# Attention and a gated feed-forward on one core: activated rows stored from ScalarE's queue, k's squares moved ahead, one sum of w_in moved back

## The chip, the core and the metric

The kernel runs on one core of a Trainium2 chip. The metric is device time in microseconds (us). The core has TensorE (PE: matmuls, with PEld for its weight loads), VectorE (DVE), ScalarE (ACT), GpSimd (POOL) and SyncE (SP), which here only issues DMAs. Each engine takes its instructions strictly in the order of the program; between engines they wait on semaphores. PSUM is the memory that TensorE writes its results to, SBUF the one that the other tensors are in.

## What is computed

Two blocks follow each other, all in float32:

```python
q_n, k_n = rmsnorm(q, g_q), rmsnorm(k, g_k)            # q, k, v: 8 batches x 12 heads x 448 x 64
scores = q_n @ k_n.T / sqrt(64)
attn = softmax(scores)
x = (attn @ v) bridged to (8*448, 12*64)               # 3584 tokens x 768
h = x @ w_in                                           # 768 x 2048
out = (h * sigmoid(h)) @ w_out                         # 2048 x 768
```

The rmsnorm divides each row of 64 by the root of its mean square (plus 1e-6) and multiplies by the gains.

## The kernel before

**Couples.** Attention goes in 24 couples of two head pairs (four heads) each, three couples per batch. Couples 0 to 5 are the first group of two batches (GROUP = 6). From couple 6 on, the feed-forward's first matmul of the group before runs between the steps of attention: couples 6 to 11 carry batches 0 and 1, couples 12 to 17 batches 2 and 3, and so on. The last group's feed-forward and the second matmul come when attention is over. From couple LATE = 12 on, q and k are loaded in another layout; some of its steps begin with couple 10 (LATE - 2).

**Visit and between.** For each couple c the program first writes `visit(c)` (L1397): the matmuls of the scores (L712), their exps on ScalarE (L717, with the norm of k as the scale), the products with v (L749), and the division of couple c - 1's result (L808). Then comes `between(c)` (L1463): the transposes of couple c + 1's q and k through TensorE (L629, L647) with their copies by ScalarE (L633, L649); the column sums of the exps, first by adds on VectorE (L763) and then by matmuls with ones (L783), their reciprocals (L792) and the DMAs that spread them (L799, L801); the norms of couple c + 2; and the filler. Exp and SiLU lie in different tables of ScalarE, so each change costs an ACT_TABLE_LOAD; `between` ends with a tiny exp (L1524) that loads exp's table again.

**The filler.** The first matmul of the feed-forward is done in blocks of seven products, as Strassen does in Winograd's form (class `Seven`, L888): for each block of 256 columns of w_in and two batches, products named 1, 2, 6, 5, 7, 3, 4 in that order (blocks 0 and 1 of the first group have 1 and 2 done earlier). A product is three matmul steps (L902) into one PSUM bank of two that are used in turn; each shows as two records in the trace. Products 1 and 5 are copied out by ScalarE (L910, L920), the others are added to something by VectorE (L857); GpSimd adds product 5 to two sums (L922, L923). A finished block leaves two rows of 128 x 896 in `stage`. When the next block has begun, `activate` (L1038) applies SiLU to both rows (L1040) and `save` (L934) stores them to `hidden` in DRAM from SyncE's queue. There are three row buffers in turn, so a later block writes a row again once its store has landed.

**fill.** `fill(others, prompt)` (L1334) writes a share of the filler's steps and deals the pieces of `others` out between them, evenly over the steps; pieces of `prompt` go after every third step. What is left comes at the end. `between` calls it twice: the first half with the late adds (L763, four pieces), rounding steps of w_in and the norms of k; the second half with rounding steps, the norms of q, and the transposes, sums and reciprocals as `prompt`. The order in `others` is the order in which the engines get the pieces.

**Norms of k** (`normalise`, L812, pieces 2 and 3): ScalarE squares one half of k's rows into a scratch tile (L467), VectorE sums them per row (L468); both halves use the same scratch, so the second square waits for the first sum; then L492 on VectorE and a power on GpSimd (L496).

**w_in.** Its 24 pieces are loaded by SyncE (L85), opened by ScalarE (L100, L101), and rounded by VectorE (L123, L126, L130) and GpSimd (L134), some in `halves` of couples, some in visits. For each of four chunks of w_in four sums (`sum_w_in`, L954, VectorE, L854 and L857 on tile W) are made ahead of the blocks that need them; `sums_halves` says in which half of which couple: `sums_halves[8]` is the first half of couple 10, index 2 (c - 6) + half.

Of the kernel before, what the change touches and what calls it, by code (L numbers as in the profile page):

```python
# [535 lines left out]
def bounded(  # L536
# [8 lines left out]
    others = ctx.enter_context(ExitStack())  # L545
# [4 lines left out]
    GROUP, LATE = z.NPAIR, z.LATE  # L550
# [3 lines left out]
    hidden = dram.tile([z.NF, P, z.B * S], F32, name="hidden")  # L554
# [9 lines left out]
    def piece(n):  # L564
        nonlocal at
        at += n
        return work[:, at - n : at]
# [17 lines left out]
    late = [extra[:, ds(2 * z.NW * S - (i + 1) * n, n)].bitcast(I32) for i in range(2)]  # L585
# [53 lines left out]
    def transpose_k(c):  # L639


        assert z.KB == BANK
        t = ps.tile([P, 2, BANK], F32, name="sc", bufs=2)
        rows = place[f"k{c % 2}"]
        for i in range(2):
            for j in range(z.KEYS + 1 - i):
                nc.tensor.transpose(t[:, i, ts(j, P)], rows[:, ds((z.KA, z.KB)[i] + j * P, P)], ident)  # L647
        columns = t.rearrange("p i s -> p (i s)")[:, 0 : z.NK]
        nc.scalar.activation(kT, columns, AF.Copy, scale=gains)  # L649
        loads["k" if c < LATE - 1 else "quarters"](min(c + 2, LATE))  # L650
# [116 lines left out]
    def sum_up(c):  # L767

        n = D // 2
        early = c < GROUP
        t = bank(S) if c < GROUP - 1 else ps.tile([P, 2, BANK], F32, name="sc", bufs=2)[:, 0, 0:S]
        terms = [(0, lambda: weights(c, 0))]
        if early:
            terms = [(0, lambda: weights(c, LEFT - 1))] + terms + [(1, None)]
        for k, (which, w) in enumerate(terms):
            if k == len(terms) - 2:
                yield  # L780
            for h in range(2):
                for i in range(2):
                    nc.tensor.matmul(  # L783
                        t[ds(h * D + i * n, n), :],
                        ones[:, which + i if which else 0],
                        eleft[:, h] if which else w()[:, i, h],
                        start=(k == 0), stop=(k == len(terms) - 1),
                    )

        def invert(half):  # L790
            rows = ts(half, S // 2)
            nc.vector.reciprocal(out=r[0][:, rows], in_=t[:, rows])  # L792

        def spread():
            mine = [a.rearrange("(h i p) s -> i h p s", h=2, i=2) for a in r]
            queues = (nc.sync, nc.gpsimd if c == GROUP - 1 else nc.sync)
            for h in range(2):
                for i in range(2):
                    queues[h].dma_start(mine[1][i, h], mine[0][1, h])  # L799
            for h in range(2):  # L800
                queues[h].dma_start(mine[0][1, h], mine[0][0, h])  # L801

        yield [lambda: invert(0), lambda: (invert(1), spread())]

    def divide(c, source):
        for i in range(2):
            x = x_of(c, i)
            nc.vector.tensor_tensor(  # L808
                out=x, in0=x if source is None else source[i], in1=r[i], op=ALU.mult
            )  # L810
# [121 lines left out]
        return stages[-1]  # L932

    def save(f, column, t):  # L934
        nc.sync.dma_start(hidden[f, :, ds(column, t.shape[1])], t)


    AHEAD = 2
# [15 lines left out]
    def sum_w_in(i, step):  # L954

        assert room.w_in.rounded >= (i + 1) * z.NW
        summed.add((i, step))
        w = room.chunk(i).rearrange("p (c m r k) -> p c m r k", c=z.NW, m=2, r=2)
        up, low = w[:, 0:HW], w[:, HW:]
        s = room.sums(i).rearrange("p (s c m k) -> p s c m k", s=3, c=HW, m=2)  # L960
        left_sums(
            up[:, :, :, 0], low[:, :, :, 0], up[:, :, :, 1], low[:, :, :, 1],
            s[:, 0], s[:, 1], s[:, 2], (step,),
        )
# [8 lines left out]
    def sum_x(group, c, steps=range(4)):  # L973
        right_sums(*quarters(group, c), *sums_of_x(c), steps)
# [359 lines left out]
    def fill(others=(), prompt=()):  # L1334


        others, prompt, steps, dealt = list(others), list(prompt), 0, 0
        if prompt:
            prompt.pop(0)()
        filler["due"] += filler["share"]  # L1340
        total = max(1, int(filler["due"] / S))
        while filler["due"] > 0:
            step = next(filler["work"], None)
            if step is None:
                break
            filler["due"] -= step
            steps += 1
            if prompt and steps % HW == 0:
                prompt.pop(0)()
            while dealt < min(len(others), len(others) * steps // total):  # L1350
                others[dealt]()
                dealt += 1
        filler["due"] = min(filler["due"], 0.0)
        for other in prompt + others[dealt:]:
            other()
# [8 lines left out]
    def finish():  # L1364
        run(filler["work"])
# [10 lines left out]
    for c in range(GROUP // 2):  # L1376
        halves[2 * (c - GROUP)], halves[2 * (c - GROUP) + 1] = "rr", "o"
    sums_halves = {-6: [(0, 0)], -4: [(0, 1)], -3: [(0, 2)], -2: [(0, 3)]}
    sums_halves[8] = [(3, step) for step in range(4)]
    sums_visits = {GROUP + 1: 1, GROUP + 3: 2}  # L1380

    def weights_in(c, half):
        i = 2 * (c - GROUP) + half
        work = [step_of[step] for step in halves.get(i, "ro" if c < GROUP else "")]
        return work + [lambda a=a: sum_w_in(*a) for a in sums_halves.get(i, ())]
# [8 lines left out]
    def last_two(c):  # L1394
        return [c // GROUP * 2 - 2, c // GROUP * 2 - 1]
# [63 lines left out]
    def run_all(work):  # L1459
        for piece in work:  # L1460
            piece()

    def between(c):  # L1463

        def transposes_and_sums():
            summing = sum_up(c)
            if c < GROUP:
                next(summing)
            if c == GROUP - 1:
                reciprocals = next(summing)  # L1470
                divide(c - 1, None)
                run_all(reciprocals)
                sum_x([0, 1], 0)
                transpose_k(c + 1)
                return
            if c < LATE - 1:
                transpose_k(c + 1)
            reciprocals = next(summing)
            if LATE - 1 <= c < NC - 1:
                reciprocals += [lambda: flip(c + 1, "k"), gain]  # L1480
            if GROUP // 2 <= c < EARLY:
                divide(c - 1, None)
            return reciprocals

        if c < LATE - 1:
            transpose_q(c + 1)
        elif c < NC - 1:
            flip(c + 1, "q")
        if c < GROUP // 2:
            inverting.extend(transposes_and_sums())  # L1490
        elif c == GROUP - 1:
            transposes_and_sums()
        if c >= GROUP and c % GROUP == 0:
            fetched = range(AHEAD) if c == GROUP else ()
            columns = products - 2 * HW * S * len(fetched)
            work = halves_in(last_two(c), range(HF), plain_in, dict(begun), fetched)
            begin(work, columns, 2 * GROUP)
            begun.clear()
        late = add(c, LEFT - 1) + add(c, LEFT) if c >= GROUP else []
        further = normalise(c + 2) if c >= GROUP - 1 else []  # L1500
        fill(late + weights_in(c, 0) + (further[2:] if c >= GROUP else further[:2]))
        prompt = transposes_and_sums() if GROUP // 2 <= c != GROUP - 1 else []
        if prompt and c < GROUP:
            prompt.insert(0, lambda: None)
        if c == GROUP // 2:
            begin(make_ahead([0, 1]), AHEAD * 2 * HW * S, GROUP - 1)
        if c >= LATE - 2:
            if c == LATE - 2:
                prompt.append(pair_up)
            queries = prompt[3:] + [lambda: sum_squares(c + 2)]  # L1510
            fill(weights_in(c, 1), prompt[:3] + [lambda: run_all(queries)])
        else:
            fill(weights_in(c, 1) + (further[:2] if c >= GROUP else []), prompt)
        if c % GROUP == GROUP - 1:
            finish()
            if c == GROUP - 1:
                begun[0] = fetch_ahead([0, 1], 0)
            elif c < NC - 1:
                sum_x([c // GROUP * 2, c // GROUP * 2 + 1], 0, range(2))
        if c >= LATE - 2:  # L1520
            scale(c + 2)
        if GROUP <= c < NC - 1:

            nc.scalar.activation(first, minus_half, AF.Exp)  # L1524
        if c == NC - 1:
            while rounder.load():
                pass
# [236 lines left out]
```

## Time and profile before

| what | us |
|---|---|
| median of three runs (lowest, highest) | 1325.13 (1323.84, 1328.43) |
| the profiled execution: whole time | 1323.7 |
| the profiled execution: span of its instructions | 1321.9 |
| TensorE busy / VectorE busy / ScalarE busy | 1298.3 / 949.2 / 505.2 |
| start of the visit of couple 7, 8, 9, 10, 11, 12 | 155.2, 189.4, 224.6, 257.9, 294.6, 327.2 |
| a store of a row (448 KB) from SyncE: median issue, median time to landing | 0.37, 3.1 |

A row of the timeline gives the start, the duration, the engine, the line, the operation, what is written and read, and in brackets how long the engine had been idle and what ended that. Times are counted from the span's start. In the list of windows each stretch is followed by its length, the busy time of TensorE, of its weight loads, of VectorE, ScalarE and GpSimd with the number of instructions, the clock granted to TensorE as a share of full speed, the mean busy share of the 16 DMA engines, and GB/s. The chain lists, in order of time, the pieces of work that released each other up to the last instruction.

### The profile page before, as it was taken

To read this page: it belongs to the slowest core of one execution; us is meant where nothing else is said; L and a number is where in the kernel's file an instruction comes from. 1 tells how busy PE (TensorE), PEld (TensorE's weight loads), DVE (VectorE), ACT (ScalarE), POOL (GpSimd) and SP (SyncE) were. 2 spreads that over 40 slices of the span, in tenths; PEclk is the share of its full clock that TensorE was granted. 3 is DMA by queue.
4 is the path that set the end of the run, shared out by engine and by line. 5 is a ranking of instruction groups with operands and counts; after the bars stand their busy time and mean duration, and the time that the engine had idled before them with its cause. 6 is when DMAs were issued, how large, how long until landed. Compare 5 with 4: busy or idle time off the path is not lost.

```text
span 1321.9 us, 19806 instructions
## 1 busy us (share of the span) xinstructions
PE 1298.3 (98%) x7193; PEld 829.3 (63%) x7193; DVE 949.2 (72%) x1629; ACT 505.2 (38%) x886; POOL 361.5 (27%) x230
## 2 busy tenths in 40 slices
PE   8989999999999999999999999999999999999998
PEld 4433444444444444444444455558999999999998
DVE  6888776776755555855554686698978787878785
ACT  7966656645545545454444253410100000001000
POOL 6756444343334334333420244410000000000000
PEclk9999999999999999999999999999999999999999
DMA  8674337233443444444321367412323232231411
GB/s 232 169 189 110 113 91 209 80 90 91 95 116 91 97 103 107 96 93 117 81 67 67 106 197 259 150 60 76 100 76 106 76 101 90 92 114 63 132 45 39
DMA packets 249439, 144.94 MB, mean 110 GB/s; under 512 B 184292, under 2 KB 233220, under 8 KB 249332
## 3 DMA queue, kind: packets, MB, share of 16 engines
q1 hardware_dynamic: 248672, 142.42, 38.5%
q8 instruction: 59, 0.97, 0.3%
q0 software_dynamic: 352, 0.96, 0.2%
q14 instruction: 48, 0.39, 0.1%
q10 hardware_dynamic: 308, 0.20, 0.1%
HBM read 93.98 MB, written 41.29 MB: 102 GB/s over the span
## 4 chain that ended last, share of the span: by engine, by line
PE 83%; DVE 6%; ACT 4%; DMA 3%; issue 2%; POOL 1%; SPq 1%; ACTq 0%; DVEq 0%; POOLq 0%
PE mm L902 25%; PE alone L1209 23%; PE mm L1209 8%; PE av L749 8%; PE sc L712 7%; PE alone L902 7%; PE alone L1246 2%; PE sc L783 1%; DMA work<-work 1%; DVE work L763 1%; DVE work L792 1%; ACT work L717 1%; PE mm L1246 1%; ACT stage L1040 1%; DMA hidden<-stage 1%
## 5 line engine op out<-in xcount | busy, mean ns | idle before, releaser
L902 PE MATMUL mm<-x,W 128*128 128x448 f32 x612 | 246.7, 546 | 4.7 <-DVE parts L857 2.0
L717 ACT ACTIVATE work<-sc,rms 128x448 f32<-128x448 f32 x324 | 184.8, 634 | 71.9 <-PE sc L712 58.0
L902 PE MATMUL mm<-sums_x,W 128*128 128x448 f32 x480 | 193.4, 543 | 1.5 <-DVE parts L857 1.5
L902 PEld LDWEIGHTS mm<-x,W 128*128 128x128 f32 x612 | 112.3, 190 | 131.1 <-issue 104.3
L712 PE MATMUL sc<-work 64*64 64x448 f32 x1344 | 165.6, 546 | 1.8 <-ACT work L717 1.5
L763 DVE TENSOR_TENSOR work<-work 128x896 f32<-128x896 f32 (+1 forms) x114 | 123.7, 1118 | 50.1 <-PE av L749 49.6
L749 PE MATMUL av<-work,rows 64*64 64x448 f32 x1296 | 154.1, 543 | 3.3 <-ACT av L725 2.2
L902 PEld LDWEIGHTS mm<-sums_x,W 128*128 128x128 f32 x480 | 89.6, 190 | 95.2 <-issue 85.5
L496 POOL TENSOR_TENSOR rms<-rms,minus_half 128x14 f32<-128x14 f32 (+4 forms) x43 | 105.2, 2449 | 149.2 <-DVE rms L492 139.6
L523 POOL DMA_DIRECT2D out_dram<-x x2 | 1.2, 594 | 443.3 <-DVE x L857 443.3
L1209 PE MATMUL alone<-W,rows 128*128 128x192 f32 x610 | 113.0, 326 | 0.0
L749 PEld LDWEIGHTS av<-work,rows 64*64 64x64 f32 x1296 | 57.8, 132 | 75.7 <-issue 35.8
L1209 PEld LDWEIGHTS alone<-W,rows 128*128 128x128 f32 x610 | 101.5, 190 | 0.0
L712 PEld LDWEIGHTS sc<-work 64*64 64x64 f32 x1344 | 53.6, 133 | 74.8 <-ACT work L717 29.2
L922 POOL TENSOR_TENSOR parts<-parts,stage 128x448 f32<-128x448 f32 x31 | 42.1, 1357 | 148.8 <-DVE parts L857 143.1
L688 POOL TENSOR_TENSOR rms<-rms,minus_half 128x28 f32<-128x28 f32 x12 | 57.5, 4794 | 64.1 <-DVE rms L685 57.4
L1209 PE MATMUL alone<-W,work 128*128 128x192 f32 x382 | 72.2, 326 | 0.0
L1040 ACT ACTIVATE stage<-stage 128x896 f32<-128x896 f32 x63 | 57.3, 945 | 23.6 <-DVE stage L857 22.9
L1219 ACT COPY rows<-alone 128x192 f32<-128x192 f32 x33 | 10.5, 319 | 142.1 <-PE alone L1209 78.4
L468 DVE TENSOR_REDUCE rms<-rows 128x8 f32<-128x512 f32 (+2 forms) x56 | 35.9, 640 | 39.1 <-ACT rows L467 37.9
L1209 PEld LDWEIGHTS alone<-W,work 128*128 128x128 f32 x382 | 63.8, 190 | 0.0
L792 DVE RECIPROCAL work<-sc 128x224 f32<-128x224 f32 x38 | 58.6, 1547 | 5.7 <-PE sc L783 5.5
(250 smaller groups left out, 2114.5 us busy)
## 6 DMA issues: line engine op xcount, KB each, us to landing
hidden<-stage SPq DMA_DIRECT2D x63, 448.0 KB, 3.1
work<-hidden SPq DMA_DIRECT2D x21, 1024.0 KB, 5.1
rows<-in_moe_w_out_dram SPq DMA_DIRECT2D x32, 384.0 KB, 3.4
W<-in_moe_w_in_dram SPq DMA_DIRECT2D x22, 512.0 KB, 5.1
work<-work SPq DMA_DIRECT2D x141, 56.0 KB, 2.0
x<-hidden SPq DMA_DIRECT2D x7, 1024.0 KB, 5.6
rows<-in_q_dram SPq DMA_DIRECT2D x96, 56.0 KB, 2.3
rows<-in_k_dram SPq DMA_DIRECT2D x96, 56.0 KB, 2.3
```

Of the source, the lines that this page charges most:

```text
L496: nc.gpsimd.tensor_tensor(out=t, in0=t, in1=half, op=ALU.pow)
L688: nc.gpsimd.tensor_tensor(out=f, in0=f, in1=minus_half.to_broadcast([P, n]), op=ALU.pow)
L712: nc.tensor.matmul(two[ds(half * D, D), h, 0:S], keys[rows, ts(half, D)], qT[rows, pair, :], start=True, stop=True,)
L717: nc.scalar.activation(eleft[:, h] if j == LEFT else weights(c, j)[:, i, h], two[:, h, 0:S], AF.Exp, scale=norm.column(c, i, h, j),)
L749: nc.tensor.matmul(sums[i][ds(h * D, D), :], v, w, start=(j == 0 and step == 1), stop=(j == LEFT - 1 and step == 1),)
L763: nc.vector.tensor_tensor(out=total, in0=total, in1=more, op=ALU.add)
L792: nc.vector.reciprocal(out=r[0][:, rows], in_=t[:, rows])
L902: nc.tensor.matmul(t, self.left(name, s), self.right(name, s), start=s == ends[0], stop=s == ends[1])
L922: nc.gpsimd.tensor_tensor(out=u2, in0=u2, in1=p5, op=ALU.add)
L1040: nc.scalar.activation(t, t, AF.Silu)
L1209: nc.tensor.matmul(t, x[:, i], y, start=i == ORDER[0], stop=i == ORDER[-1])
L1246: nc.tensor.matmul(o, a[:, 2 * i + m, t], right_one(name, i)[:, m], start=n == 0, stop=n == len(steps) - 1,)
```

## The change

Three edits. `save` uses ScalarE's queue where the column is 0, which is the first group, whose blocks are made in couples 6 to 11: sixteen stores. In the first half of couples 6 to 10 the two pieces of k's squares stand ahead of the adds and rounding steps. Of the four sums of w_in's last chunk the fourth goes to the second half of couple 10; empty pieces keep the number of pieces of its first half at ten, and set its place in the second.

```diff
     def save(f, column, t):
-        nc.sync.dma_start(hidden[f, :, ds(column, t.shape[1])], t)
+        queue = nc.scalar if column == 0 else nc.sync
+        queue.dma_start(hidden[f, :, ds(column, t.shape[1])], t)
...
-    sums_halves[8] = [(3, step) for step in range(4)]
+    sums_halves[8] = [(3, step) for step in range(3)]
+    sums_halves[9] = [(3, 3)]
...
-        fill(late + weights_in(c, 0) + (further[2:] if c >= GROUP else further[:2]))
+        others = late + weights_in(c, 0)
+        rest = further[2:] if c >= GROUP else further[:2]
+        others = rest + others if GROUP <= c < LATE - 1 else others + rest
+        if c == LATE - 2:
+            others.append(lambda: None)
+        fill(others)
...
-            fill(weights_in(c, 1), prompt[:3] + [lambda: run_all(queries)])
+            steps = weights_in(c, 1)
+            fill(steps + [lambda: None] * len(steps), prompt[:3] + [lambda: run_all(queries)])
```

The stores on ScalarE stand in its order right behind the SiLU of their row, one between the two SiLUs of a block and one behind them. In couples 6, 7, 9 and 10 both squares of k reach ScalarE ahead of the block's SiLUs; in couple 8 the first does and the second comes behind the two SiLUs and their stores. TensorE's order is the same in both programs.

## The prediction

> **What bounds the kernel now.** I read the page's busy times first, then six windows from the end of one couple's scores to the start of the next couple's, then the chain and the timelines inside them.
>
> ```profile
> PE 1298.3 (98%) x7193; PEld 829.3 (63%) x7193; DVE 949.2 (72%) x1629; ACT 505.2 (38%) x886; POOL 361.5 (27%) x230
> ```
>
> TensorE is the bound: 98%, so all idle time together is 1321.9 - 1298.3 = 23.6 us. The windows of couples 6 to 11 (columns: stretch, then length, then busy time of each engine):
>
> ```profile
> 132.10:155.20 23.10, 22.73 (x83) 11.30 (x79) 19.48 (x29) 13.00 (x19) 8.62 (x7) 1.00 0.33 93
> 166.20:189.40 23.20, 22.58 (x79) 11.34 (x79) 16.72 (x25) 12.84 (x20) 7.35 (x5) 1.00 0.46 128
> 200.40:224.50 24.10, 22.93 (x76) 11.16 (x75) 17.11 (x22) 13.06 (x20) 8.39 (x6) 1.00 0.73 211
> 235.60:257.80 22.20, 22.20 (x76) 11.37 (x75) 16.93 (x22) 12.50 (x20) 7.64 (x5) 1.00 0.28 68
> 269.70:294.60 24.90, 23.28 (x85) 11.57 (x81) 19.87 (x22) 10.29 (x14) 9.55 (x9) 1.00 0.48 111
> 305.60:327.20 21.60, 21.36 (x66) 10.05 (x65) 15.54 (x19) 9.17 (x12) 4.81 (x3) 1.00 0.46 113
> ```
>
> TensorE idles 139.10 - 135.09 = 4.0 us in them; 0.9 us more is idle inside the visits of couples 10 and 12. That is the whole prize. The clock is full (1.00). The largest stall, couple 8, in the chain of waits:
>
> ```profile
> 204.77 1.79 ACT stage L1040 x2
> 206.56 0.08 ACT W L100
> 206.63 5.32 DMA hidden<-stage
> ...
> 212.49 0.64 ACT rows L467
> ...
> 213.15 0.70 DVE rms L468
> ...
> 213.87 0.53 ACT rows L467
> ...
> 215.19 0.88 DVE work L792
> ...
> 216.57 0.57 DVE parts L857
> ```
>
> ScalarE's copy of product 5 (L920) may not write the stage row until its save has landed; k's squares (L467) stand behind it, VectorE's reduces (L468) behind those, and L857, which empties the bank that TensorE wants, behind all. ScalarE at 38% is idle on average, yet at the end of couple 9 it is the chain:
>
> ```profile
> 253.81 1.79 ACT L1040 ACTIVATE stage<-stage 128x896 f32<-128x896 f32 x2
> 255.51 0.66 ACT L100 ACTIVATE W<-W 128x512 int32<-128x512 uint32 x1
> ...
> 257.74 0.61 ACT L467 ACTIVATE rows<-rows 112x512 f32<-112x512 f32 x1
> 259.10 0.63 ACT L467 ACTIVATE rows<-rows 112x512 f32<-112x512 f32 x1 [0.75 <-DVE rms L468]
> 259.75 1.28 ACT L1524 ACT_TABLE_LOAD   x1
> 261.15 1.14 ACT L717 ACTIVATE work<-sc,rms 128x448 f32<-128x448 f32 x2
> ```
>
> Couple 10's scores start at 257.87, their exps only at 261.15, and TensorE stalls at 261.86 for 0.49 us. Exps may start 2.4 us after the scores at no cost: that visit takes 11.85 us with a delay of 3.28, the other visits of couples 6 to 11 take 11.0 with delays near 1.1 to 1.8.
>
> **Yardsticks.** A 3-step product is 6 TensorE records 0.376 apart, 2.26 us. Products alternate between two PSUM banks, so the copy or sum that empties one has one product's time. A stall costs its idle time plus about 0.17 for the drained pipeline and 0.10 at restart. TensorE's order is unchanged by the change; its times move only through waits.
>
> **Part 1, saves on ScalarE's queue.** Sixteen issues leave SyncE (0.32 to 1.36 us each, median 0.37) and go to ScalarE. The trace has five ScalarE issues of other tensors: 0.53, 0.23, 0.54, 0.50, 0.39; I take 0.44, bounds 0.23 and SyncE's 1.24 in couple 8. Each waits for its SiLU, and the second SiLU stands behind the first issue. A pair of SiLUs takes 1.79 now; with two gaps of 0.06, two issues, and the 0.10 of overlap lost, about 2.9: **+1.1 us of ScalarE per pair** (bounds +0.7, +2.7). Queued behind it: L100/L101, k's or q's squares, the table load and the next exps.
>
> There is a second wait. The built program hands out eight landing semaphores in turn, so a transfer waits for the landing of the one eight before it in program order. On SyncE's in-order queue this cost little; now ScalarE stands still for it. For most saves the earlier transfer landed long ago. Two do not: couple 8's first save follows the w_in load issued at 201.86, which lands between 205.26 and 207.26 (its neighbours' landings), I take 207.0; couple 6's second save follows the w_in load of 143.37.
>
> Couple 9: +1.1 on the chain shown, exps delayed 4.4: +1.1 us. Couple 11: SiLUs 313.71 to 315.50, squares 315.41, reduces, reciprocal 318.00, L857 ending 320.03, TensorE at 320.08 already stalled: no cover, +1.1. Its second pair ends in the table load of 328.84; the second SiLU waits for L857 anyway, so one issue counts: +0.5.
>
> What the move removes: couple 10's save was issued at 289.75, 2.4 us after its SiLU, because SyncE was issuing q and k quarters; L920 waited 3.92 for it and TensorE 0.72 at 292.75. Issued at about 286.6 it has landed when product 5 ends at 290.5: gain 0.72 + 0.16, and the smaller waits of 0.12 and 0.10 ahead of it go too. DMA queues share: couple 8's window moves 211 GB/s with a share of 0.73, and its save took 5.32 to land.
>
> The Trainium skill, "DMA: Bandwidth & Descriptors", section "Issuing engines are not separate DMA queues", speaks against expecting faster landings: transfers from any engine run on the same 16 DMA engines and interleave, and only issue time is saved. By it the change frees 16 x 0.37 us of a queue that bounds nothing. Saves landing in 2.5 rather than 5.3 us would change no term here, as the rows are rewritten later in either case.
>
> **Part 2, k's squares first.** Couple 7: now L792 (179.74 to 181.29) stands before L857 and delays it; with the squares done L792 starts at 178.65, right after the ones matmul, and L857 ends near 180.75, before TensorE wants the bank at 180.88: **-0.9** (0.62 idle plus drain and restart). Its own pair of saves is hidden, as ScalarE waits for product 5 till 181.05.
>
> Couple 6: ScalarE reaches the first square only after L633 (136.66), so it ends at 137.2; VectorE has finished two adds at 135.61 and stands idle for the reduce (137.25 to 137.95). Product 6's sum moves from 136.53 to 137.9, ends 138.5, TensorE wants that bank at 137.46: +1.1. The old stall of 0.36 at 142.13 goes, but the reciprocals shift by about 1.4 and product 6 of the next block stalls 0.4 to 0.9. Sum **+1.2** (0 to +2.5; the upper end if the second save's load, which now also waits for the adds that were moved ahead of the rounding on GpSimd, lands after 153).
>
> Couple 8, the largest term. In the new order ScalarE has: first square, L910, table load, SiLU, save, SiLU, save, **second square**; and VectorE has the second reduce before an add and before the sum of product 2. By rows: first square ends 203.0, L910 203.55, load 204.83, SiLU 205.78, wait to 207.0, issue 207.4, SiLU 208.35, issue 208.8, square 209.35; reduce 0.56, L492 0.17, add 1.08, L857 0.61: 211.8. TensorE wants that bank at 207.23: a stall of 4.6. From there to the next visit are 15.6 us without stalls (17.32 now, less 1.76), so it starts at 227.5 rather than 224.55: **+2.95**. The second pair delays the next exps from 1.83 to 3.2 after the scores: +0.7. Without the semaphore wait and with issues of 0.23 the two are +1.4 and +0.3.
>
> Couple 9: the squares come early without a stall; nothing waited there: 0. Couple 10: two reduces and L492 (1.4 us) come before product 7's sum, which moves from 275.62 to 276.7 against 275.82: a new stall of 0.95; product 3's sum ends at 279.3 instead of 279.09: +0.2 net.
>
> **Part 3, the sum of w_in.** One of four sums (0.94) moves behind product 6's sum. It gives room before product 4's sum, already in the 0.2; later VectorE waits for L672 and for product 7, which hides it. If it weren't hidden: +0.9.
>
> **Sum.** 6: +1.2; 7: -0.9; 8: +3.65; 9: +1.1; 10: +0.2 - 1.1 = -0.9; 11: +1.6. Total **+5.8 us**. On the profiled execution (span 1321.9, 1323.7 with what lies around it) that is 1329.5. The three runs' median, 1325.13, is 1.4 above that execution, and a median is what I forecast: 1330.9.
>
> **Rivals.** (a) Light issues: 0.23 us, no semaphore wait, couple 6 at +0.5: 0.5 - 0.9 + 1.7 + 0.7 - 1.0 + 1.0 = +2.0, 1327.1. For it: ScalarE's shortest issue; against: the other four. (b) Heavy issues: each like SyncE's 1.24 and 0.93 in couple 8, 1.3 more per pair at five places (one of them half): about +11.6, 1336.7. For it: that window's DMA share; against: issues elsewhere are 0.32 to 0.42. (c) Faster: the squares take the landing out of couples 7, 8 and 10 and the second square doesn't delay product 2; the gains alone are 0.9 + 1.76 + 1.1 + 0.5 = 4.3, 1320.8. It decides at one point: couple 8's second reduce before 205.3. Against it stands the built order: table load 1.28 and SiLUs 1.79 lie between. (d) The saves don't leave SyncE: excluded, the built program has sixteen on ScalarE.
>
> **How the numbers follow.** Forecast 0.60, (a) 0.23, (b) 0.11, (c) 0.06. Range 1325.5 to 1336: from +0.4 to +10.9, leaving out (c) and the far half of (b). About 0.3% (4.0 us) is what a measurement tells from no change. Faster: half of (c), 0.03. Same: the other half, (a), and 0.08 of the forecast, 0.34. Slower: 0.63.
>
> **What would show it.** Right: in couple 8 a TensorE stall of 3 to 5 us before product 5, ended by L857 behind the 128x6 reduce; ScalarE issues of 0.4 to 0.5; visit 10's first exps over 4 us after its scores; no wait of L920 for hidden. Wrong: ScalarE issues that cost next to nothing, or the second square ahead of the SiLUs in time.

## The result, and the profile after

The changed kernel takes 1332.83 us (median of six runs, 1330.48 to 1334.62), the kernel before 1323.88 in the same comparison: ratio 1.0063, 95% interval 1.0052 to 1.0074. It is slower by 8.9 us. The forecast was 1330.9, with a range of 1325.5 to 1336.0.

The profiled execution is the longest of the six: 1334.62, span 1332.8. TensorE's busy time grew by 3.3 us (1298.3 before) though it runs the same instructions, and its idle time by 7.6 (from 23.6 to 31.2). The first of these was no part of the forecast; 2.4 us of it arise in couple 8, and most of the rest lies ahead of the change (below). The page:

```profile
PE 1301.6 (98%) x7193; PEld 829.5 (62%) x7193; DVE 952.3 (71%) x1629; ACT 506.8 (38%) x886; POOL 366.4 (27%) x230
```

The windows of couples 6 to 11, from the end of a couple's scores to the start of the next couple's (columns as before):

```profile
133.69:158.83 25.14, 23.13 (x80) 11.10 (x76) 20.35 (x27) 11.42 (x17) 9.71 (x6) 1.00 0.38 112
169.97:192.20 22.23, 22.23 (x76) 11.21 (x75) 17.21 (x26) 13.34 (x20) 7.34 (x5) 1.00 0.46 134
203.19:232.60 29.41, 25.29 (x77) 12.48 (x76) 16.98 (x22) 12.69 (x19) 9.15 (x6) 0.88 0.60 172
244.30:266.53 22.23, 22.23 (x75) 11.34 (x76) 15.84 (x22) 11.89 (x18) 8.94 (x5) 1.00 0.37 101
279.44:304.12 24.68, 23.01 (x83) 11.66 (x80) 18.86 (x22) 11.02 (x15) 8.42 (x8) 1.00 0.50 117
315.58:337.89 22.31, 21.02 (x62) 9.79 (x60) 15.11 (x19) 9.06 (x12) 4.82 (x3) 1.00 0.43 108
```

Couple 7 has no idle time of TensorE left (22.23 of 22.23). Couple 8 takes 29.41 in place of 24.10, with 4.12 idle, 2.4 more busy time and a clock of 0.88 where each of these windows had 1.00 before. The timeline of couple 8 shows the new order at work (start, duration, engine; in brackets the idle time ahead and what ended it):

```profile
205.15 0.65 ACT L467 ACTIVATE rows<-rows 128x512 f32<-128x512 f32 x1
...
206.28 1.28 ACT L1041 ACT_TABLE_LOAD   x1
...
207.58 0.95 ACT L1041 ACTIVATE stage<-stage 128x896 f32<-128x896 f32 x1
...
209.62 0.35 ACTq L936 DMA_DIRECT2D hidden<-stage  x1
210.02 0.95 ACT L1041 ACTIVATE stage<-stage 128x896 f32<-128x896 f32 x1 [1.49 <-DMA x<-in_moe_w_in_dram]
211.00 0.33 ACTq L936 DMA_DIRECT2D hidden<-stage  x1
211.43 0.52 ACT L467 ACTIVATE rows<-rows 128x384 f32<-128x384 f32 x1 [0.46 <-ACT stage L1041]
211.98 0.55 DVE L468 TENSOR_REDUCE rms<-rows 128x6 f32<-128x384 f32 x1 [5.47 <-ACT rows L467]
...
213.66 0.62 DVE L857 TENSOR_TENSOR stage<-mm,stage 128x448 f32<-128x448 f32 x1
...
214.33 1.11 PE L902 MATMUL mm<-sums_x,W 128*128 128x448 f32 x1 [4.12 <-DVE stage L857]
```

The first SiLU ends at 208.53, but its store is issued only at 209.62, when a load of w_in has landed. The second SiLU, the second store and the second square follow. VectorE, idle for 5.47 us, gets its second reduce at 211.98 and its sum at 213.66, and TensorE starts product 5 at 214.33 after 4.12 us. That product then runs slowly: its six records take 4.85 us, where those of product 6 took 2.42. Stretches of couple 8 (the last three columns are clock, DMA share, GB/s):

```profile
209.54:212.95 3.41, 0.67 (x2) 0.00 (x0) 0.93 (x3) 1.47 (x2) 0.06 (x1) 1.00 1.29 265
212.95:216.37 3.42, 2.04 (x3) 1.17 (x4) 3.42 (x5) 0.00 (x0) 3.23 (x1) 0.50 0.93 363
216.37:219.78 3.41, 3.41 (x6) 1.41 (x5) 1.52 (x2) 0.56 (x2) 0.00 (x0) 0.50 0.03 9
219.78:223.19 3.41, 3.41 (x21) 1.72 (x20) 1.94 (x4) 2.43 (x4) 0.54 (x1) 1.00 0.01 2
```

From 212.95 to 219.78 the granted clock is 0.50. TensorE worked in 5.45 us of that (from 214.33), so it lost about 2.7 us.

To place the rest, each TensorE instruction's start was set against that of the same instruction in the trace of before. The table gives by how much the lateness grew within each couple (a couple's exps that start late are counted with the couple that delayed them). "Stores alone" and "squares alone" are two of the experiments below.

| couple | forecast | changed kernel | stores alone | squares alone |
|---|---|---|---|---|
| 6 | +1.2 | +2.07 | 0.00 | +2.04 |
| 7 | -0.9 | -0.84 | +0.51 | -0.84 |
| 8 | +3.65 | +5.84 | +0.49 | +2.06 |
| 9 | +1.1 | +1.06 | +1.03 | 0.00 |
| 10 | -0.9 | -0.17 | -1.11 | +1.18 |
| 11 | +1.6 | +1.56 | +1.56 | 0.00 |
| sum | +5.8 | +9.5 | +2.5 | +4.4 |

The profiled execution was already 1.59 us late when couple 6 began: its stall at 68.9, which lies in a part that the change doesn't touch, was 3.50 instead of 2.05, and the clock stood at 0.50 behind it, from 73.01 to 76.42. That is a difference of executions; what made the stall longer stays open. The growth of 9.5 in the table is therefore that of one execution, the longest.

### The profile page after: what moved, and what is told of

Its sections match the earlier page's. It is cut to its first block, busy times and chain, and to the rows that moved or that the text cites. A ratio compares the mean times of both kernels' runs of the same rounds, so it can differ in the third digit from the quotient of the medians.

```text
span 1332.8 us, 19789 instructions
## 1 busy us (share of the span) xinstructions
PE 1301.6 (98%) x7193; PEld 829.5 (62%) x7193; DVE 952.3 (71%) x1629; ACT 506.8 (38%) x886; POOL 366.4 (27%) x230
## 4 chain that ended last, share of the span: by engine, by line
PE 82%; DVE 6%; ACT 4%; DMA 2%; issue 2%; POOL 1%; SPq 0%; ACTq 0%; DVEq 0%; POOLq 0%
PE mm L902 26%; PE alone L1210 22%; PE mm L1210 8%; PE alone L902 7%; PE av L749 7%; PE sc L712 7%; PE alone L1247 2%; PE sc L783 1%; DMA work<-work 1%; ACT work L717 1%; DVE work L763 1%; ACT stage L1041 1%; DVE work L792 1%; DMA W<-in_moe_w_in_dram 1%; PE mm L1247 1%
## 5 line engine op out<-in xcount | busy, mean ns | idle before, releaser
L496 POOL TENSOR_TENSOR rms<-rms,minus_half 128x14 f32<-128x14 f32 (+4 forms) x43 | 108.1, 2517 | 177.0 <-DVE rms L492 164.7
L922 POOL TENSOR_TENSOR parts<-parts,stage 128x448 f32<-128x448 f32 x31 | 42.8, 1380 | 136.9 <-DVE parts L857 136.7
```

The lines of the kernel that those rows point to most:

```text
L496: nc.gpsimd.tensor_tensor(out=t, in0=t, in1=half, op=ALU.pow)
L922: nc.gpsimd.tensor_tensor(out=u2, in0=u2, in1=p5, op=ALU.add)
```

## The experiments

The theory after the result: stores and squares each have a price or a gain in a place of its own, and only in couple 8 do they meet, because the second square stands behind SiLUs, stores and a landing there; TensorE's stall of 4.1 us then lowers its clock. Rivals: the issues on ScalarE cost all of it wherever they stand; or product 5 is slow because 300 GB/s of transfers pass at that time. All ratios are against before, in five rounds, with 95% intervals; each is uncertain by about 0.1%, 1.3 us, so differences between two experiments under some 2 us aren't told apart by the times alone.

**Stores alone.** Before with the first edit only:

```diff
-        nc.sync.dma_start(hidden[f, :, ds(column, t.shape[1])], t)
+        queue = nc.scalar if column == 0 else nc.sync
+        queue.dma_start(hidden[f, :, ds(column, t.shape[1])], t)
```

> Before with the first edit alone: the sixteen stores on ScalarE's queue; the squares of k and the sums of w_in as before. Against before. Theory (each edit has its own place): couple 6 keeps the part that came from the wait for a landing on ScalarE's queue, +0.5 to +1; couple 8 has SiLUs and squares about 2 us later on ScalarE with the old order, its stall of 1.17 grows to 2 to 3 and the exps of the next visit are 0.7 late, together +1.5 to +2.5; couple 9 +0.7; couple 10 loses the stall behind its store, -0.9; couple 11 +1.5. Sum about +4 us, ratio near 1.003; no stall over 3 us and TensorE's granted clock stays at 1.00 through couple 8. Rival (the issues are the cost, and the new order of the squares is harmless): +7 to +9 us, as much as the whole change.

Measured: 1.0012 (1.0003 to 1.0021), 1.6 us. The rival falls, and the theory's sum of about 4 us was too high: couple 6 cost nothing where 0.5 to 1 was expected, and couple 8 came out better than either theory had it (+0.49). Couple 7, which the theory leaves out, took 0.51. In couple 8 the first store waits too, but k's squares stand behind product 5's copy in this order and VectorE isn't kept from its sum:

```profile
206.11 0.95 ACT L1041 ACTIVATE stage<-stage 128x896 f32<-128x896 f32 x1
...
208.16 0.35 ACTq L936 DMA_DIRECT2D hidden<-stage  x1
...
208.56 0.95 ACT L1041 ACTIVATE stage<-stage 128x896 f32<-128x896 f32 x1 [1.50 <-DMA x<-in_moe_w_in_dram]
```

**Squares alone.** Before with the second edit only:

```diff
-        fill(late + weights_in(c, 0) + (further[2:] if c >= GROUP else further[:2]))
+        others = late + weights_in(c, 0)
+        rest = further[2:] if c >= GROUP else further[:2]
+        fill(rest + others if GROUP <= c < LATE - 1 else others + rest)
```

> Before with the second edit alone: k's squares ahead of the adds in couples 6 to 10; the stores stay on SyncE and the sums of w_in as before. Against before. Theory: couple 6 +1; couple 7 -0.8; couple 8: the second square stands behind the table load and two SiLUs, but no store and no landing, so the stall before product 5 is about 2.3 us (4.1 less two issues of 0.35 and a wait of 1.09) against the 1.17 it replaces, +0.7 to +1.2, and the clock stays full; couple 10 +0.9; couples 9 and 11 nothing. Sum about +2 us, ratio 1.0015. If a stall of 2.3 us also lowers the clock, +4 to +5. Rival (the order of the squares is harmless, and the stores cost all): -1 to 0.

Measured: 1.0025 (1.0014 to 1.0036), 3.3 us. Couples 6 and 7 come out as in the changed kernel (+2.04 and -0.84), couple 9 takes nothing and couple 10 takes 1.18. Couple 8's stall is 1.95 us, 2.2 less than with the stores (the wait of 1.09, two issues of 0.34 and gaps). Yet the stretch after it is at half clock; the first column after the stretch's length is TensorE's busy time:

```profile
206.14:209.56 3.42, 1.47 (x5) 0.56 (x4) 2.58 (x5) 0.77 (x2) 1.71 (x1) 1.00 1.27 262
209.56:212.97 3.41, 3.41 (x6) 1.39 (x6) 3.29 (x4) 0.00 (x0) 1.58 (x1) 0.50 1.04 398
```

Of couple 8's +2.06, about 1.7 (half of 3.41) is this stretch. "The clock stays full" was wrong.

**Sums alone.** Before with the third edit only:

```diff
-    sums_halves[8] = [(3, step) for step in range(4)]
+    sums_halves[8] = [(3, step) for step in range(3)]
+    sums_halves[9] = [(3, 3)]
...
+        if c == LATE - 2:
+            others.append(lambda: None)
...
+            fill(steps + [lambda: None] * len(steps), prompt[:3] + [lambda: run_all(queries)])
```

> Before with the third edit alone: one of the four sums of w_in's last chunk goes to the second half of couple 10. Against before. Theory (hidden, VectorE waits there for TensorE anyway): 0 within 0.5 us, the stalls of couple 10 as before. Rival (not hidden): +0.9 us, a stall before product 3 or 4 in the second half of couple 10.

Measured: 0.9997 (0.9988 to 1.0006). Hidden, as forecast: the stalls of couple 10 are 0.89 and 0.72, as in before.

**The stall filled with matmuls.** In the changed kernel, couple 8's product 6 is issued two or three times (the loop shown runs over its steps once, or twice):

```diff
+            if name == "6" and twice.pop(now["c"], False):
+                for s in self.steps:
+                    nc.tensor.matmul(
+                        t, self.left(name, s), self.right(name, s),
+                        start=s == ends[0], stop=s == ends[1],
+                    )
```

> The changed kernel, with the three matmul steps of product 6 of couple 8 issued twice into the same bank, which fills 2.26 us of the 4.12 us in which TensorE stands before product 5; the result is the same and nothing waits for it longer. Theory (the granted clock falls because TensorE stands still for 4 us): the stall shrinks to about 1.9 us, product 5 takes 2.3 us again instead of 4.6, the clock stays at 1.00 and the kernel is 2.8 us faster than the changed one although it does more: about +6 us on before, ratio 1.0045. Rival (product 5 is slow because of the DMA traffic of 301 GB/s in that stretch, or is merely recorded so): as the changed kernel, +9 us, ratio 1.0065, or up to 2 us more.

Measured: 1.0072 (1.0058 to 1.0086), no faster. It didn't decide: SyncE issued w_in's load later against ScalarE's squares than in the changed kernel, the first store waited 1.2 us longer for it, and a stall of 3.02 was left, with one stretch at half clock in place of two. So it was done with more:

> The changed kernel, with the matmul steps of product 6 of couple 8 issued three times into the same bank (4.5 us more for TensorE in the place of its stall); the result is the same. The run with the steps twice still had a stall of 3.02 us, as the first store waited 1.2 us longer for a landing, and its clock was at half for one stretch of 3.41 us in place of two. Theory (the clock goes to half for a stretch of 3.41 us when TensorE stood for about half or more of the stretch before): with less than 1 us left of the stall no stretch of couple 8 is at half, product 5 takes 2.3 us, and the whole is 1.5 to 2.7 us faster than the changed kernel in spite of 4.5 us more of matmuls: +6.3 to +7.8 on before, ratio 1.005 to 1.006. Rival (the matmuls of product 5 are slowed by the transfers of that stretch): product 5 still takes 4.6 us, +9 to +9.5, ratio 1.007.

Measured: 1.0041 (1.0028 to 1.0054). By the ratios the kernel that runs 4.5 us more of matmuls is 2.9 us faster than the changed one (0.0022 of 1325); the two intervals just touch, so the size is rough. The traces agree with it: couple 8 grows by 2.66 us here, by 5.23 in the changed kernel. No stretch of couple 8 is at half, though the transfers are the same:

```profile
206.90:210.39 3.49, 3.49 (x10) 1.71 (x9) 0.38 (x1) 1.47 (x2) 0.00 (x0) 1.00 1.27 268
210.39:213.80 3.41, 3.41 (x11) 1.73 (x10) 3.38 (x7) 0.00 (x0) 2.88 (x1) 1.00 1.03 388
```

The second stretch holds product 5 at full clock beside 388 GB/s, so it isn't the transfers that slow it. TensorE's standing still is shown as the cause.

**Couple 8's first two stores back on SyncE**, all else as in the changed kernel (c is 8 in the first half of couple 8's `between` alone):

```diff
-        queue = nc.scalar if column == 0 else nc.sync
+        queue = nc.scalar if column == 0 and now["c"] != 8 else nc.sync
```

> The changed kernel, but the two stores in the first half of couple 8 are on SyncE's queue. Theory (two issues of 0.35 and a wait of 1.1 for a landing stand ahead of the second square): the second square follows the second SiLU at once, the stall falls from 4.1 to about 2.0 us and the clock loses one stretch at half or none: 2 to 5 us faster than the changed kernel, +4 to +7 on before, ratio 1.003 to 1.005. Rival (table load and SiLUs alone make the stall): stall as before it, about 4 us, +8 to +9.

Measured: 1.0047 (1.0032 to 1.0063), by the ratios 2.1 us less than the changed kernel, with intervals that overlap. The stall is 1.95, as in "squares alone": issues and landing make 2.2 us of the 4.1, and the rival falls. In its profiled run the clock stayed full, and couple 8 then cost only +0.37; with the stretch at half it was 2.06 in "squares alone". Counted in steps of 3.413 from the fall that this trace has at 127.14, a border between stretches lies at 209.06 and divides the stall (208.30 to 210.25) into 0.76 and 1.19. The six times of this kernel range from 1327.8 to 1334.0, with mean granted clocks from 0.998 to 0.993; only the first was profiled, so what the others lost in couple 8 isn't known.

**Couple 8 in the old order**, stores on ScalarE:

```diff
-        others = rest + others if GROUP <= c < LATE - 1 else others + rest
+        others = rest + others if GROUP <= c < LATE - 1 and c != 8 else others + rest
```

> The changed kernel, but in couple 8 alone k's squares stand where they stood before, behind the adds and rounding steps; the stores stay on ScalarE. Theory (in couple 8 the place of the second square behind SiLUs and stores makes the stall, and the stall makes the clock fall): the stall of 4.1 us and the slow product 5 (2.8 us) go, the old stall behind the landing of the store comes back with 1.2 to 3 us: 3.5 to 5.5 us faster than the changed kernel, +3.5 to +5.5 on before, ratio 1.003 to 1.004, clock 1.00. Rival (the stores alone hold ScalarE up, wherever the squares stand): as the changed kernel within 1 us, +8 to +9.5.

Measured: 1.0020 (1.0011 to 1.0029), 5.7 us faster than the changed kernel, a little better than expected: the old stall came back with only 0.74, the clock stayed full in couple 8, and the rival falls. Here the first store waits for the landing as in the changed kernel (its SiLU ends at 208.94, it is issued at 210.02).

**Both squares as one first piece in couple 8**, all else as in the changed kernel:

```diff
+        both = [lambda: run_all(rest)] if c == 8 else rest
-        others = rest + others if GROUP <= c < LATE - 1 else others + rest
+        others = both + others if GROUP <= c < LATE - 1 else others + rest
```

> The whole changed kernel, but in couple 8 the two squares of k are one first piece, so that the second too stands ahead of the table load, the SiLUs and the stores. Theory (one piece in the wrong place makes the largest loss): the stall of 4.1 us and the two stretches at half clock go, 4.1 + 2.7 less up to 1.6 for the later stalls that come back = 5 to 7 us faster than the changed kernel, +2 to +4 on before, ratio 1.002 to 1.003. Rival (the first store's wait for a landing stalls TensorE in couple 8 anyway, as product 5's row and the next copies stand behind it on ScalarE): at most 3 us faster than the changed kernel, +6.

Measured: 1.0019 (1.0009 to 1.0029). Couple 8 alone falls from +5.23 to +0.06, without the late exps that follow it (0.61 in the changed kernel, 0.53 here). In this run the first store also finds its landing done (its SiLU ends at 207.35, it is issued at 207.38), so by itself it doesn't separate the square's place from the landing. Together with the run before, which has the landing's wait and is as fast, it shows what makes most of the loss: VectorE's second reduce stands ahead of product 2's sum while its square stands behind the SiLUs and stores. With the square ahead of them, or the reduce behind that sum, the loss is gone.

**Only what gained.** Before, with both squares first in couples 7 and 8 and ScalarE's queue in couple 10 alone:

```diff
-        nc.sync.dma_start(hidden[f, :, ds(column, t.shape[1])], t)
+        queue = nc.scalar if now["c"] == 10 else nc.sync
+        queue.dma_start(hidden[f, :, ds(column, t.shape[1])], t)
...
-        fill(late + weights_in(c, 0) + (further[2:] if c >= GROUP else further[:2]))
+        others = late + weights_in(c, 0)
+        rest = further[2:] if c >= GROUP else further[:2]
+        if c in (7, 8):
+            fill([lambda: run_all(rest)] + others)
+        else:
+            fill(others + rest)
```

> Before with only the pieces that gained: in couples 7 and 8 both squares of k as one first piece, so that in couple 8 the second square too stands ahead of the table load and the SiLUs; stores on ScalarE's queue in couple 10 alone; sums of w_in as before. Against before. Theory: couple 7 -0.8, couple 8 -1.5 (its stall of 1.17 behind the landing of the store, and the small ones after it), couple 10 -0.9: -3.2 us, ratio 0.9976. Rival (two squares ahead of product 1's copy hold up its bank or the sum of product 2): couple 8 no better than before or worse, -1.7 to +1 us in all.

Measured: 0.9983 (0.9974 to 0.9992). By lateness couples 7, 8 and 10 give 0.58 + 0.13 + 0.99 = 1.7 us, the near end of the rival's range and not the theory's 3.2, but not for the rival's reason. Couple 8 didn't gain: as two pieces had become one, the opening of w_in (L100, L101) slid behind product 5's copy (L920), which waits for the landing of the store. VectorE's rounding (L123) waited for it, with the reciprocal and the sum of product 7 behind, which TensorE's product 4 wanted (the last row; the next text calls it the stall before product 3):

```profile
211.38 0.53 ACT L920 COPY stage<-mm 128x448 f32<-128x448 f32 x1 [4.36 <-DMA hidden<-stage]
211.81 0.67 ACT L100 ACTIVATE W<-W 128x512 int32<-128x512 uint32 x1
...
213.07 0.43 DVE L123 TENSOR_SCALAR W<-W 128x512 f32<-128x512 f32 x1 [3.61 <-ACT W L101]
...
216.69 0.64 PE L902 MATMUL mm<-sums_x,W 128*128 128x448 f32 x1 [1.45 <-DVE parts L857]
```

So the opening was put back where it stood:

```diff
+        if c == 8:
+            adds, opening, rounding = others[:4], others[4], others[5:]
+            fill([lambda: run_all(rest)] + adds[:3] + [lambda: run_all([adds[3], opening])]
+                 + rounding + [lambda: None] * 2)
...
```

> As the run with only the gaining pieces, but in couple 8 the opening step of w_in (L100, L101) stands again ahead of product 5's copy, as it did before; in that run it had slid behind the copy, which waits for the store's landing, and took the place of the squares behind it: the stall before product 3 stayed, 1.45 us. Against before. Theory (the stall of couple 8 is whatever ScalarE has queued behind the landing): now nothing but the copy of k is behind it, the stall of couple 8 goes, and couples 7, 8 and 10 give 0.7 + 1.3 + 1.1 = 3.1 us: ratio 0.9977. Rival (the landing itself holds TensorE up, whatever is queued behind it): a stall of 1 us or more stays in couple 8, -2 us, ratio 0.9984, as the run before it.

Measured: 1320.25 us, 0.9961 (0.9948 to 0.9975): faster than both kernels. No stall of 1 us is left in couple 8, so the rival falls. The windows of couples 7, 8 and 10 hold 22.49, 22.60 and 22.97 us of busy time in 22.49, 22.86 and 23.86:

```profile
167.12:189.61 22.49, 22.49 (x76) 11.12 (x75) 16.65 (x25) 13.20 (x20) 8.05 (x5) 1.00 0.47 132
200.60:223.46 22.86, 22.60 (x77) 11.35 (x76) 17.08 (x22) 12.92 (x19) 9.16 (x6) 1.00 0.81 225
268.63:292.49 23.86, 22.97 (x84) 11.63 (x80) 19.84 (x22) 10.91 (x15) 8.54 (x8) 1.00 0.48 113
```

By lateness the three give 0.57 + 1.32 + 0.99 = 2.9 us; the ratio says 5.2, its near end 3.3. The other 2 us may be a difference of executions or not; that stays open.

**Couple 10.** There the squares alone cost 1.18 where 0.2 was forecast. The rows of the changed kernel name a queue that the forecast left out, GpSimd's:

```profile
284.80 3.29 POOL L496 TENSOR_TENSOR rms<-rms,minus_half 128x14 f32<-128x14 f32 x1 [4.07 <-DVE rms L492]
...
286.10 2.08 DVE L763 TENSOR_TENSOR work<-work 128x896 f32<-128x896 f32 x2
...
288.06 1.12 POOL L922 TENSOR_TENSOR parts<-parts,stage 128x448 f32<-128x448 f32 x1
...
289.21 0.62 DVE L857 TENSOR_TENSOR stage<-mm,parts 128x448 f32<-128x448 f32 x1 [1.03 <-POOL parts L922]
...
289.89 2.52 PE L902 MATMUL mm<-x,W 128*128 128x448 f32 x6 [1.13 <-DVE stage L857]
```

The power of k's norm (L496), which came forward with the squares, stands ahead of GpSimd's sum of product 5 (L922). VectorE waits 1.03 for that sum, and TensorE 1.13 (the last row is product 1 of the next block, which waits for product 3's sum; the texts below call it the stall before product 3). In before the power came only at 284.65, behind both of GpSimd's sums (275.77 and 277.70). To test it, the root was moved to the end of the half:

```diff
+    last = []
...
-            elif i == 1:
+            elif i == 1 and c == LATE and name == "k":
+                last.append(lambda: norm.root(c, name))
+                loads["k"](c + 1)
+            elif i == 1:
                 norm.root(c, name)
...
-            others.append(lambda: None)
+            others.append(lambda: run_all(last))
```

The first form leaves out the line `loads["k"](c + 1)`, and with it the load of k for couple 13, so it doesn't compute the same result.

> The changed kernel, but in couple 10 the last step of k's norm (VectorE's L492 and GpSimd's power of 3.3 us behind it) is a piece of its own at the end of the first half; the squares and their row sums stay in front. Theory (the power, moved with the squares, stands ahead of GpSimd's sum of product 5 (L922), VectorE's sum behind it starts 1.0 us late, and TensorE's next product waits for that): the stall before product 3 of couple 10, 1.13 us, falls to 0.3 or less, the one before product 7 (0.54) falls by at most the 0.17 of L492; the whole is 0.8 to 1.2 us faster than the changed kernel, +7.5 to +8.5 on before. Rival (the stall comes from VectorE's row sums alone, 1.4 us ahead of all its later work): the 1.13 stay within 0.2.

Measured: 1.0055 (1.0042 to 1.0069), and a stall of 0.94 where 0.3 was expected. The time is the expected one, but not for the expected reason: couple 8, which this edit doesn't touch, has a stall of 4.19 here and only one stretch at half clock, and grows by 4.31 in place of 5.23.

> As the run with the root of couple 10 last, with the load of k for couple 13 in its place (that run left it out). That run's stall before product 3 of couple 10 was 0.94 us and not 0.3: GpSimd's sum of product 5 came early, but beside it two of VectorE's adds took 3.02 us in place of 2.08, so VectorE reached its own sum late all the same. Theory now (a wait for GpSimd has become a slower VectorE beside GpSimd; the row sums put ahead are what VectorE is short of): stall 0.9 to 1.0, adds again near 3.0, the whole 0.2 to 0.5 us faster than the changed kernel, within what a measurement tells. Rival (the missing load had changed the stretch): stall 0.3 or 1.13, adds near 2.1.

Measured: 1.0068 (1.0054 to 1.0082), the stall 0.94 again. The sum now comes early, at 284.90 (the line numbers are a few higher in this kernel), but VectorE's two adds beside it take 3.02 in place of 2.08, and its own sum starts right after them:

```profile
284.67 3.02 DVE L763 TENSOR_TENSOR work<-work 128x896 f32<-128x896 f32 x2
...
284.90 1.84 POOL L927 TENSOR_TENSOR parts<-parts,stage 128x448 f32<-128x448 f32 x1 [5.39 <-DVE parts L862]
...
286.71 1.97 POOL L928 TENSOR_TENSOR stage<-parts,stage 128x448 f32<-128x448 f32 x1
287.62 0.61 DVE L862 TENSOR_TENSOR stage<-mm,parts 128x448 f32<-128x448 f32 x1
```

The first theory falls in its size: the wait was real, but taking it away shortened this stall by 0.19 only, as the two engines slow each other. The stall before product 4 fell from 0.54 to 0.34, and couple 10 as a whole gave 0.39 by lateness, which is too little for the times to tell. That what couple 10 lacks is VectorE's time, as its row sums (1.2 us) now stand ahead of its other sums, is argued from the rows; no run took them apart.

## Why the prediction was right, and where not

**The bound and the side: right.** TensorE at 98% was the bound and the added waits showed as its stalls. The time is 1.9 us above the forecast, inside the range. That it is so near is in part luck: the forecast stood on before's first median, 1325.13, where the comparison has 1323.88, so the growth was missed by 3.1 us (8.9 for 5.8). The growth in the traces is 9.5, the forecast 5.8; the 3.7 lie in three couples: 8 (+2.2), 6 (+0.9) and 10 (+0.7).

**Part 1, issues and landing: right, the issues priced a little high.** Issues on ScalarE took 0.33 to 0.37 where 0.44 was taken. The landing wait in couple 8 came as described, 1.09 where 1.2 was forecast (205.78 to 207.0). Couples 9 (+1.06 for +1.1) and 11 (+1.56 for +1.6) fit. Couple 9's chain is as forecast, 4.35 us from the scores at 266.53 to the first exp where 4.4 was said:

```profile
269.47 1.28 ACT L1532 ACT_TABLE_LOAD   x1
...
270.88 1.66 ACT L717 ACTIVATE work<-sc,rms 128x448 f32<-128x448 f32 x3
```

The gain in couple 10 is confirmed by the stores alone: -1.11, forecast -1.1. No wait of L920 for `hidden` is left in couples 6 to 11; before had two, 8.3 us in all. Couple 6's second store did wait for the w_in load, issued at 155.00 where its SiLU had ended at 152.33, but the stores alone cost couple 6 nothing.

**Part 2, couple 7: right** (-0.84 for -0.9).

**Couple 8: mechanism right, one term missing.** The stall was forecast as 4.6, it was 4.12; its net price was 5.23 - 2.73 = 2.5 where 2.95 was said, the late exps 0.61 where 0.7 was said. What failed is the line "The clock is full (1.00)": it was read from the windows of before and carried over to a kernel with a longer stall. The term that was missing is about 2.7 us in the profiled execution; that the standing still makes it is shown by "the stall filled". It isn't a fixed price: in the first form of the run on couple 10's root a stall of 4.19 us, which lies otherwise to the borders of the stretches, cost one stretch and not two. How much of it is in the median isn't known. The trace of before held the row. At 119.70, ahead of the change, TensorE stands for 1.97 us, and the next stretch has the clock at half:

```profile
118.35:121.77 3.42, 1.45 (x20) 0.41 (x16) 3.35 (x6) 1.89 (x5) 0.78 (x2) 1.00 0.08 21
121.77:125.18 3.41, 3.41 (x20) 1.20 (x24) 3.34 (x6) 1.50 (x4) 3.29 (x2) 0.50 0.56 129
```

**Couple 6: mis-sized, inside its bounds** (+2.07; 1.2 forecast, up to 2.5). The new stall was 0.95 (1.04 forecast), but two stalls followed, 0.43 and 0.63. The second, behind product 6's sum, had been forecast as 0.4 to 0.9; the first, behind product 3's sum, had not. VectorE's rounding, which now meets GpSimd's additions, took 1.25 a piece where 0.43 was its time before:

```profile
145.61 1.25 DVE L123 TENSOR_SCALAR W<-W 128x512 f32<-128x512 f32 x1
...
146.54 1.32 POOL L923 TENSOR_TENSOR stage<-parts,stage 128x448 f32<-128x448 f32 x1
...
146.90 1.25 DVE L126 TENSOR_SCALAR W<-W 128x512 int32<-128x512 int32 x1
```

That these 1.6 us of delay make the two later stalls is argued from the order of the rows; no run took them apart.

**Couple 10: the step that failed is "+0.2 net".** The squares cost 0.94 there, the -0.17 of the changed kernel less the -1.11 of the stores alone. The first new stall was 0.54 (0.95 forecast), but the old one of 0.90 grew to 1.13 instead of shrinking. Product 3's sum ended at 289.83, which is 280.1 on the clock of before (9.72 less), where 279.3 was forecast. GpSimd's queue wasn't followed: the power stood ahead of its sum of product 5.

**Part 3: right,** hidden.

**The rivals.** Light issues (1327.1) needed 0.23 us each and no wait, heavy issues (1336.7) 1.24 and 0.93; the issues took 0.33 to 0.37, and the wait came. The faster case was said to turn on couple 8's second reduce before 205.3. In the two kernels of "only what gained" it begins at 203.53 and 204.52, and both are faster than before. But that point alone doesn't decide: in "both squares as one first piece" it begins at 204.70, and that kernel is slower than before, as couples 6, 9 and 11 still cost 2.06, 1.07 and 1.56.

## What to carry to other kernels

When a change can lengthen a stall of the bound engine, look in the trace for the longest stall that it already has and at the granted clock right after it; here stalls near 2 us were paid a second time, as a stretch at half clock, when they fell into one stretch. Moving a step moves its part on every engine: here the square's row sums held up VectorE and its power GpSimd, and one square behind two SiLUs and their stores, with its reduce early in VectorE's order, cost more than all the stores alone. Pieces that are dealt out by count change places when two are merged, so look again at what stands behind each landing.

## What the runs showed of the hardware

**TensorE's clock goes by stretches of 3.41 us.** In 14 profiles every fall of the granted clock ahead of the last matmuls is to 0.50 and lasts one or two such stretches, and in one profile the falls lie whole multiples of 3.41 apart (in the changed kernel's at 73.01, 124.21 and 212.95). Of the stretches in which TensorE stood for more than 1.2 us at full clock (its ends are modelled; each trace's first stretch and the last matmuls are left out), none of 18 with up to 1.74 us was followed by one at half, and 18 of 20 with 1.78 to 3.16 us were. The limit isn't the same everywhere: of 13 first stretches that stood as long, the four longest, with 1.55 to 1.62 us, were followed by one at half. So a stall of 2 us mostly costs 1.7 us more when it falls into one stretch, and nothing more when a border divides it: before's stall of 2.05 at 68.92 had 1.64 in one stretch, and the clock stayed at 1.00. A stall of 4.19 us with 3.03 of it in one stretch and the rest ahead of that cost one stretch (first form of the run on couple 10's root); one of 4.12 that reached 1.38 into the stretch at half cost two (changed kernel).

The Trainium skill, "TensorE: Matmul & The Clock Gate", section "Part 1: The HAM clock gate (the "warmup" mystery)", states the free-running window (3413 ns) and the two rates, with which these rows agree. Its section "HAM oscillation — how this bites in real kernels" gives the rule as no idle gaps over about 3.4 us; by it the stall of 1.95 in "squares alone" would have cost nothing more, where the row shows 3.41 us at half clock. Here the measurement decides: about half a stretch was enough.

**VectorE and GpSimd slow each other.** Beside GpSimd's additions, VectorE's 128x512 rounding took 1.25 for 0.43 and two adds 3.02 for 2.08; GpSimd's own addition took 1.84 to 1.97 in place of 1.12. Putting the two side by side instead of one behind the other took 0.19 off a stall of 1.13.
